# Output products in phases of their own, block products in two interleaved chains, and Strassen's seven products for the output GEMM of two superblocks

## The chip, the cores and the metric

One Trainium2 chip, one of its cores. The metric is the device time of one execution in microseconds (us): the median of three runs before the change is 983.1 us (982.56 to 983.92).

## The reference, cut to what matters

Causal window attention (window 64) over 4 x 576 tokens with 8 heads of 64, then a gated MLP with RMS norm, then a second MLP. 2304 tokens of width 512 go through all of it:

```python
xn = x / rms * rms_g
silu = g * (1.0 / (1.0 + np.exp(-g)))      # g = xn @ w_gate, 512 -> 1536
x = silu * (xn @ w_val) @ w_out            # 1536 -> 512
h = x @ w_in                               # 512 -> 2048
out = (h * (1.0 / (1.0 + np.exp(-1.702 * h)))) @ w_out2   # 2048 -> 512
```

The inputs are 64-bit floats; the kernel converts the weights on the chip from their 32-bit halves.

## The kernel before, in words

**Numbers.** Every GEMM keeps its operands as a high and a low fp32r part and does three matmuls for one (high x high, low x high, high x low).

**Stage 1** (loop `for j in range(NB)`, six blocks of 384 tokens): attention of the next block runs beside the first half of the gated MLP of this block, f = 0 to 5: `psg` and `psv` (12 matmuls of 384 columns each, helper `proj`), then 12 into the four `acc` banks (`emit_O`). At a block's end the next block's x is split into `xh` and `xl` (`split_x`, L462 to L466), on which the next `psg` waits.

**Stage 2** (three superblocks of 768 tokens, p = 0 to 2): the second half of the gated MLP. g and v come from Strassen's seven products of 2 x 2 blocks (Winograd's form with few sums): `chain` does 7 x 6 matmuls of 384 columns into two banks, `psa` and `psb`. ACT copies bank `psa` (`snap`, L677), DVE adds bank `psb` (`plus`, L681); `fill` puts groups of 12 output matmuls of the previous p between some of the products (`half_groups`: 6 of 512 and 6 of 256 columns on the same weights).

**Stage 3** (three superblocks, f = 0 to 7): the second MLP. h by the same `chain`, gelu and split into `g` (L936 to L938), and the output GEMM as plain matmuls of 512 columns into six banks, 36 for each f, put between the products as groups of 9 (`out_groups`).

**Weights.** `w_step` converts one pair of weight tiles: L201 and L202 on ACT (128x1024 each), L203, L204 and L207 on DVE (`m`). `w_half` then splits it; where Strassen's products need them, `w_products` makes four differences (L149 to L152) and high and low parts (`whi` L157, `wlo` L158, three pieces each) and stores them to DRAM, from where `t_load` brings `wt` back (two tiles for each chain). The conversions of stage 2 and 3 run on ACT and DVE beside the stage before.

**Order.** From the second block on the order of TensorE's instructions is that of the program; ACT, DVE and the DMA queue on SP take theirs from a scheduler, and each runs its own list strictly in order. A tile's buffer comes from a pool and is taken again when its last reader is done. The core of `chain` before:

```python
            a = mm_p.tile([128, 512], F32, tag="g", name="psa")
            prod(a, 0, True)
            s1 = snap("al")
            fill(0)
            b = mm_p.tile([128, 512], F32, tag="v", name="psb")
            prod(b, 1, True)
            prod(a, 5, False)
            plus(s1)
            s2 = snap("al")
            take(0, s1)
            fill(1)
            b = mm_p.tile([128, 512], F32, tag="v", name="psb")
            prod(b, 6, True)
            prod(a, 4, False)
```

Of the kernel before, what the change touches and what calls it, by code (L numbers as in the profile page):

```python
# [22 lines left out]
def window_attention__gated_mlp__mlp_kernel(  # L23
# [13 lines left out]
    nc = tc.nc  # L37
# [16 lines left out]
    wp = ctx.enter_context(tc.tile_pool(name="wp", bufs=11))  # L54
    const = ctx.enter_context(tc.tile_pool(name="const", bufs=1))
    xp = ctx.enter_context(tc.tile_pool(name="xp", bufs=4))
    ap_ = ctx.enter_context(tc.tile_pool(name="ap", bufs=2))
# [72 lines left out]

    def w_load(limit):
        while w_next[0] < min(limit, n_w):
            pair = w_order[w_next[0]]
            w_next[0] += 1
            st = stp.tile([128, 2, 1024], I32, tag="st", name="st")
            for e, (kind, f) in enumerate(pair):
                dst = st[:, e, :].rearrange("p (k f) -> p k f", k=KC) if kind in "gvh" else st[:, e, :]
                nc.sync.dma_start(out=dst, in_=w_src(kind, f))
            staged.append(st)
# [4 lines left out]
    wd = {}  # L144

    def w_products(key, m):
        b11, b21, b12, b22 = (m[:, i * 256:(i + 1) * 256] for i in range(4))
        t = mt[0][:, 1, :].bitcast(F32).rearrange("p (b c) -> p b c", c=256)
        nc.vector.tensor_tensor(t[:, 0, :], b12, b11, ALU.subtract)  # L149
        nc.vector.tensor_tensor(t[:, 1, :], b22, t[:, 0, :], ALU.subtract)  # L150
        nc.vector.tensor_tensor(t[:, 2, :], b22, b12, ALU.subtract)
        nc.vector.tensor_tensor(t[:, 3, :], b21, t[:, 1, :], ALU.subtract)  # L152
        hi = wp.tile([128, 7, 256], F32R, tag="w", name="whi")
        lo = wp.tile([128, 7, 256], F32R, tag="w", name="wlo")
        for dst, src in ((slice(0, 2), m[:, 0:512]), (slice(2, 3), m[:, 768:1024]), (slice(3, 7), t)):
            src = src if src is t else src.rearrange("p (b c) -> p b c", c=256)
            nc.scalar.copy(hi[:, dst, :], src)  # L157
            nc.vector.tensor_tensor(lo[:, dst, :], src, hi[:, dst, :].bitcast(F32), ALU.subtract)  # L158
        d = dram.tile([128, 2, 7, 256], F32, name="w%s_%d" % key, tag="w%s_%d" % key)
        nc.sync.dma_start(out=d[:, 0], in_=hi.bitcast(F32))  # L160
        nc.sync.dma_start(out=d[:, 1], in_=lo.bitcast(F32))
        wd[key] = d

    mt = [None]

    def w_half():
        if not half:
            return
        pair, w24 = half.pop()
        kind, p = pair[0]  # L170
        paired = kind == pair[1][0] and p + 1 != pair[1][1]
        if paired and kind in "gvh":
            return w_products(pair[0], w24.bitcast(F32))
        w = wp.tile([128, 2, 1024], F32R, tag="w", name="w")
        nc.scalar.copy(w[:, 0, :], w24.bitcast(F32))
        nc.vector.tensor_tensor(w[:, 1, :], w24.bitcast(F32), w[:, 0, :].bitcast(F32), ALU.subtract)
        if paired:
            d = dram.tile([128, 2, 1024], F32, name=f"w{kind}_{p}", tag=f"w{kind}_{p}")
            nc.sync.dma_start(out=d, in_=w.bitcast(F32))
            wd[kind, p] = d  # L180
            weights[kind, p] = w
            return
        for e, key in enumerate(pair):
            weights[key] = w[:, :, e * 512:(e + 1) * 512]

    def w_step(limit):
# [8 lines left out]
        if w_next[1] <= n_wh:  # L195
            m = wp.tile([128, 1024], I32, tag="w", name="m")
        else:
            mt[0] = stp.tile([128, 2, 1024], I32, tag="st", name="m")
            m = mt[0][:, 0, :]
        with after(hold[0]):  # L200
            nc.scalar.mul(hi.bitcast(F32), hi.bitcast(F32), 2.0 ** -112)  # L201
            nc.scalar.activation(lo, lo.bitcast(U32), AF.Copy, scale=2.0 ** -29)  # L202
        nc.vector.tensor_scalar(m.bitcast(U32), hi.bitcast(U32), 3, None, ALU.logical_shift_left)  # L203
        nc.vector.scalar_tensor_tensor(  # L204
            m.bitcast(U32), hi.bitcast(U32), 0x80000000, m.bitcast(U32), ALU.bitwise_and, ALU.bitwise_or
        )
        nc.vector.tensor_tensor(m, m, lo, ALU.add)  # L207
        half.append((pair, m))
        w_load(w_next[1] + 2)
# [22 lines left out]
    def part_tile():  # L232
        if not quad:
            pool = qp if n_quads[0] < 3 else wp
# [322 lines left out]
    if True:  # L557
# [55 lines left out]
        def small(tag):  # L613
            return ap_.tile([128, TB], F32, tag=tag, name=tag)

        MADE = (0, 1, 5, 6, 4, 2, 3)
        W_OF = (0, 1, 2, 6, 3, 4, 5)

        def x_raws(src):
            r = [x1p.tile([128, KC, TB], F32, tag="xr", name="xr", bufs=2) for _ in range(2)]  # L620
# [4 lines left out]
        def x_split(src):  # L625
            t = x1p.tile([128, 2, 2, TB], F32R, tag="xop", name="xop", bufs=8)
            nc.scalar.copy(t[:, 0], src)
            nc.vector.tensor_tensor(t[:, 1], src, t[:, 0].bitcast(F32), ALU.subtract)
            return t

        def x_first(r):
            a11, a12, a21, a22 = r[0][:, 0:2, :], r[0][:, 2:4, :], r[1][:, 0:2, :], r[1][:, 2:4, :]
            ops = {0: x_split(a11)}
            u, v = (osp.tile([128, 2, TB], F32, tag="os", name="xs") for _ in range(2))
            nc.vector.tensor_tensor(u, a21, a22, ALU.add)
            nc.vector.tensor_tensor(a21, a11, a21, ALU.subtract)
            nc.vector.tensor_tensor(a11, u, a11, ALU.subtract)
            nc.vector.tensor_tensor(v, a12, a11, ALU.subtract)
            return ops, {1: a12, 5: a11, 6: a21, 4: u, 2: v, 3: a22}

        def x_next(ops, left):
            for i in MADE:
                if i in left:
                    ops[i] = x_split(left.pop(i))
                    return
# [7 lines left out]
        def o_load(key):  # L653
            w = wp.tile([128, 2, 1024], F32R, tag="w", name="wo")
            nc.sync.dma_start(out=w.bitcast(F32), in_=wd[key])
            return w

        def chain(w, xo, fill, take, used):
            def prod(ps, i, first):
                k = 0  # L660
                for wi, xi in ((0, 0), (1, 0), (0, 1)):
                    for c in range(2):
# [3 lines left out]
                            w[wi][:, W_OF[i], c * 128:(c + 1) * 128],  # L666
# [6 lines left out]
                used(i)  # L673

            def snap(tag):
                t = small(tag)
                nc.scalar.copy(t, a[:, :TB])  # L677
                return t

            def plus(t):  # L680
                nc.vector.tensor_tensor(t, t, b[:, :TB], ALU.add)  # L681
                return t

            a = mm_p.tile([128, 512], F32, tag="g", name="psa")
            prod(a, 0, True)
            s1 = snap("al")
            fill(0)
            b = mm_p.tile([128, 512], F32, tag="v", name="psb")
            prod(b, 1, True)
            prod(a, 5, False)  # L690
            plus(s1)
            s2 = snap("al")
            take(0, s1)
            fill(1)
            b = mm_p.tile([128, 512], F32, tag="v", name="psb")
            prod(b, 6, True)
            prod(a, 4, False)
            s4 = snap("s")
            plus(s4)
            take(3, s4)  # L700
            fill(2)
            prod(a, 2, False)
            prod(b, 3, False)
            take(1, a[:, :TB])
            plus(s2)
            take(2, s2)
            fill(3)

        for j in range(NB):
# [28 lines left out]
            for f in range(FH):  # L738
# [13 lines left out]
                ah = ap_.tile([128, TB], F32R, tag="ah", name="ah")  # L752
                al = ap_.tile([128, TB], F32R, tag="al", name="al")
# [18 lines left out]
                if f == 0 and end:  # L772
                    at_es.close()
                    x1p = ctx.enter_context(tc.tile_pool(name="x1p", bufs=1))
                    raws = x_raws(lambda e: xd[e])
                if f == 1 and end:
                    xo, left = x_first(raws)
                if f > 1 and end:
                    for _ in range(2):
                        x_next(xo, left)  # L780
# [16 lines left out]

        pinned[0] = True
        nothing = lambda *_: None
        groups = [late.pop(), nothing, nothing, nothing]  # L800
        PIECES = ((0, 512), (512, 2 * TB))
        wg, wv, wo = t_load(("g", FH)), t_load(("v", FH)), o_load(("o", FH))

        def half_groups(sb, p, g, wo):
            if p == 0:
                banks = [(acc_p, f"acc{c}") for c in range(4)] + [(atp, "att")] * 2
                accs = [pool.tile([128, 512], F32, tag=tag, name="acc") for pool, tag in banks]
                spots[sb] = [(accs[c], accs[4 + c // 2][:, (c % 2) * 256:(c % 2 + 1) * 256]) for c in range(KC)]
            todo = [(e, c, pi, k) for e in (1, 0) for c in range(KC) for pi in range(3) for k in range(2)]

            def group(lo):
                for e, c, pi, k in todo[lo:lo + 12]:
                    first = p == 0 and e == 1 and pi == 0
# [165 lines left out]
```

## Time and profile before

| | |
|---|---|
| median of 3 runs | 983.1 us |
| the profiled execution | 981.57 us |
| its span, first to last instruction | 979.8 us |
| busy share of the span: TensorE (PE) / DVE / ACT | 96% / 58% / 51% |
| chain that ended last: PE / DVE / DMA / ACT | 78% / 8% / 5% / 5% |
| first block product of stage 2 starts | 363.68 us |
| first output product of stage 3 starts | 602.28 us |
| last matmul group starts | 965.21 us |

PE's matmuls overlap, and the profile models their ends: the step from one to the next is read from the starts of two groups in the order of time, not from the mean duration of one. A wait is idle time of an engine with the instruction that ended it.

### The profile page before, as it was taken

The page shows a single profiled execution, that of the slowest core. Times are in us where ns is not written, and L with a number is a line of the kernel's source. Part 1 is how long each engine was busy: PE and PEld are TensorE (multiplying, and loading weights), DVE is VectorE, ACT ScalarE, POOL GpSimd, SP SyncE. Part 2 cuts the span into 40 slices and gives each one's busy share as a digit, 9 for nine tenths or more (in the row PEclk, how much of TensorE's full clock was granted, in tenths as well). Part 3 has the DMA queues.
Part 4 walks back from the last instruction along what each step waited for, and adds up shares of the span by engine and source line. Part 5 has one row for each costly group of instructions (what it writes and reads, how often), then busy time and mean ns, then how long its engine had stood idle before and what let it go on. Part 6 is the DMA issues. An engine that isn't in the chain of part 4 may idle for free.

```text
span 979.8 us, 15502 instructions
## 1 busy us (share of the span) xinstructions
PE 937.7 (96%) x5966; PEld 859.7 (88%) x5966; DVE 571.8 (58%) x1207; ACT 495.0 (51%) x1054; POOL 12.2 (1%) x39
## 2 busy tenths in 40 slices
PE   8889999999999897999999989999999999999998
PEld 7789898989989897988988979888888888888887
DVE  5898578577776875677777676645452223422222
ACT  7786566556564344464464365545543333523332
POOL 2000000000000000000000000000000000000000
PEclk9899899999999899999999999999999999999999
DMA  9956376746655589899999898776583535554301
GB/s 223 255 161 175 109 194 179 218 121 194 193 162 186 187 329 412 325 398 385 359 371 352 337 382 316 264 269 246 193 315 139 233 135 220 209 210 172 151 1 65
DMA packets 136074, 228.95 MB, mean 234 GB/s; under 512 B 79936, under 2 KB 106560, under 8 KB 131392
## 3 DMA queue, kind: packets, MB, share of 16 engines
q1 hardware_dynamic: 135472, 227.96, 66.8%
q8 instruction: 47, 0.77, 0.3%
q14 instruction: 27, 0.22, 0.1%
q10 hardware_dynamic: 528, 0.00, 0.0%
HBM read 171.84 MB, written 56.10 MB: 233 GB/s over the span
## 4 chain that ended last, share of the span: by engine, by line
PE 78%; DVE 8%; DMA 5%; ACT 5%; issue 2%; SPq 2%; POOL 0%; ACTq 0%; DVEq 0%
PE acc L92 32%; PE psa L92 16%; PE psb L92 12%; PE psg L92 6%; PE psv L92 6%; DMA wt<-wv 2%; PE ps_v L92 2%; ACT st L201 1%; SPq L266 1%; PE ps_s L92 1%; ACT st L202 1%; DMA st<-in_moe_w_val_dram 1%; PE ps_t L92 1%; DMA wo<-wo 1%; PE ps_r L92 1%
## 5 line engine op out<-in xcount | busy, mean ns | idle before, releaser
L92 PE MATMUL psa<-xop,wt 128*128 128x384 f32 x1008 | 206.2, 340 | 8.2 <-ACT al L677 6.5
L92 PEld LDWEIGHTS psa<-xop,wt 128*128 128x128 f32 x1008 | 177.6, 188 | 17.3 <-ACT al L677 9.1
L92 PE MATMUL psb<-xop,wt 128*128 128x384 f32 x756 | 155.0, 340 | 6.6 <-DVE al L681 5.1
L92 PEld LDWEIGHTS psb<-xop,wt 128*128 128x128 f32 x756 | 134.5, 188 | 13.7 <-DVE al L681 7.5
L92 PE MATMUL acc<-wo,g 128*128 128x512 f32 x576 | 144.4, 397 | 0.0
L92 PEld LDWEIGHTS acc<-wo,g 128*128 128x128 f32 x576 | 107.7, 188 | 21.1
L681 DVE TENSOR_TENSOR al<-al,psb 128x384 f32<-128x384 f32 x84 | 46.4, 553 | 123.0 <-PE psb L92 118.3
L938 DVE TENSOR_TENSOR g<-a,g 128x384 fp32r<-128x384 f32 x96 | 53.1, 556 | 58.7 <-ACT g L937 58.7
L92 PE MATMUL acc<-g,wo 128*128 128x512 f32 (+1 forms) x432 | 81.8, 337 | 0.3 <-DVE g L865 0.3
L92 PE MATMUL psg<-xh,w 128*128 128x384 f32 x288 | 69.5, 366 | 7.0 <-DVE xh L462 3.4
L92 PEld LDWEIGHTS acc<-g,wo 128*128 128x128 f32 x432 | 68.1, 188 | 8.6 <-DVE g L865 0.6
L92 PE MATMUL acc<-w,g 128*128 128x512 f32 x288 | 72.3, 397 | 0.0
L677 ACT COPY al<-psa 128x384 f32<-128x384 f32 x84 | 39.9, 475 | 53.6 <-PE psa L92 53.5
L681 DVE TENSOR_TENSOR s<-s,psb 128x384 f32<-128x384 f32 x42 | 23.2, 552 | 72.2 <-ACT s L677 72.2
L677 ACT COPY s<-psa 128x384 f32<-128x384 f32 x42 | 20.1, 479 | 86.6 <-PE psa L92 86.6
L92 PEld LDWEIGHTS acc<-w,g 128*128 128x128 f32 x288 | 53.9, 188 | 10.4
L92 PE MATMUL psv<-xh,w 128*128 128x384 f32 x288 | 62.3, 349 | 0.0
L92 PEld LDWEIGHTS psg<-xh,w 128*128 128x128 f32 x288 | 51.5, 197 | 11.2 <-DVE xh L462 4.9
L92 PE MATMUL acc<-ah,w 128*128 128x384 f32 x288 | 60.0, 344 | 0.0
L362 ACT ACTIVATE p<-p,sm 128x128 f32<-128x128 f32 x128 | 49.6, 394 | 17.0 <-DVE sm L350 17.0
L936 ACT ACTIVATE a<-al 128x384 f32<-128x384 f32 x48 | 25.2, 526 | 60.7 <-DVE al L681 59.3
L92 PEld LDWEIGHTS psv<-xh,w 128*128 128x128 f32 x288 | 52.1, 193 | 0.3 <-issue 0.2
(129 smaller groups left out, 1369.4 us busy)
## 6 DMA issues: line engine op xcount, KB each, us to landing
wt<-wh SPq DMA_DIRECT2D x48, 896.0 KB, 6.7
wo<-wp SPq DMA_DIRECT2D x16, 1024.0 KB, 4.7
wt<-wg SPq DMA_DIRECT2D x18, 896.0 KB, 10.8
wt<-wv SPq DMA_DIRECT2D x18, 896.0 KB, 8.9
st<-in_moe_w_out_dram SPq DMA_DIRECT2D x28, 512.0 KB, 4.4
xr<-x SPq DMA_DIRECT2D x12, 768.0 KB, 6.2
wo<-wo SPq DMA_DIRECT2D x9, 1024.0 KB, 10.4
st<-in_moe_w_in_dram SPq DMA_DIRECT2D x16, 512.0 KB, 6.9
```

The source lines that it names most:

```text
L92: ins = op(*args, **kw)
L201: nc.scalar.mul(hi.bitcast(F32), hi.bitcast(F32), 2.0 ** -112)
L202: nc.scalar.activation(lo, lo.bitcast(U32), AF.Copy, scale=2.0 ** -29)
L266: nc.sync.dma_start(out=t[off:off + n], in_=src[b, :, s:s + n, :].rearrange("h s d -> s h d"))
L362: last_exp[0] = nc.scalar.activation(p[e][:, hp, :], p[e][:, hp, :], AF.Exp, bias=sm[:, 0, i:i + 1], scale=-1.0, accum_out=sm[:, 1, i:i + ...
L677: nc.scalar.copy(t, a[:, :TB])
L681: nc.vector.tensor_tensor(t, t, b[:, :TB], ALU.add)
L936: hold[0] = nc.scalar.activation(a, c, AF.Gelu_apprx_sigmoid).ins
L938: nc.vector.tensor_tensor(g[1][:, q, :], a, g[0][:, q, :].bitcast(F32), ALU.subtract)
```

## The change

- **Output products as phases.** `fill` is gone. `put` gives every piece of work a key, and `run_items` runs the pieces by key. One step (one product, 6 matmuls) is one key apart from the next.
- **Two chains.** `chain` is a generator that stops after each product; chain n+1 starts 7 keys after chain n, and a product of one alternates with a product of the other. Odd chains use the two `att` banks, even ones the `mm` banks. The order of the seven products is new, with two running sums.
- **Stage 2.** The output GEMM has units of 12 or 6 matmuls of 384 columns, for tokens t = 1, then t = 0; all six `w_out` tiles stay on the core (`wo`); p runs forwards, backwards, forwards, so that a turn finds its weights loaded.
- **Stage 3.** The first superblock keeps plain output matmuls of 512 columns, one chain with pieces between its steps. In the second and third the output GEMM is seven products too (`out_products`): 28 units of 18 matmuls of 256 columns, each on an operand that `prep` makes (a sum in place, a cast on ACT, a difference on DVE) four units ahead, and on weight blocks that `wload` reads from DRAM, 1 MB each, 14 for a superblock. The first three and, in the second superblock, the last three units lie between steps of chains.
- **Conversions.** In stages 2 and 3 the sign is kept by a Prelu on ACT, and the `or` on DVE (L204) is gone; `whi` is one cast, `lo` one difference, written over the staging tile `m`. The `w_out` pairs move from stage 1 into stage 2's first superblock.
- **Pools.** 11 buffers `wp` become 7 and 4 `wr`; stage 2 and 3 have their own pools of `g`.

```diff
-    wp = ctx.enter_context(tc.tile_pool(name="wp", bufs=11))
+    wp = ctx.enter_context(tc.tile_pool(name="wp", bufs=7, side="right"))
+    wr = late_es.enter_context(tc.tile_pool(name="wr", bufs=4, side="right"))
...
-    for p in range(NP1):
-        w_order += [((kind, FH + p), (kind, FH + NP1 + p)) for kind in "gvo"]
-    n_w1 = len(w_order)
+    for kinds in ("gv", "o"):
+        for p in range(NP1):
+            w_order += [((kind, FH + p), (kind, FH + NP1 + p)) for kind in kinds]
+        if kinds == "gv":
+            n_w1 = len(w_order)
...
+        hi = spare[0].tile([128, n, 256], F32R, tag="w", name="whi")
+        m = t[:, 0:n]
+        lo = lo_pool[0].tile([128, n, 256], F32R, tag="wl", name="wlo") if kind == "p" else m.bitcast(F32R)
+        nc.scalar.copy(hi, m)
+        nc.vector.tensor_tensor(lo, m, hi.bitcast(F32), ALU.subtract)
...
+                nc.scalar.activation(hi.bitcast(F32), hi.bitcast(F32), AF.Prelu, scale=2.0 ** -112, alpha=-(2.0 ** 32))
...
+            a = bank(n, 0)
+            prod(a, 0, True)
+            s1 = snap(a)
+            yield
+            b = bank(n, 1)
+            prod(b, 6, True)
+            s7 = snap(b)
+            yield
+            prod(a, 5, False)
+            s2 = snap(a)
+            yield
+            prod(b, 3, False)
+            take(2, plus(s2, b))
+            yield
...
+                for k in range(7):
+                    put(t0 + 14 * (n // 2) + 7 * (n % 2) + 2 * k, step)
...
+                if total:
+                    nc.vector.tensor_tensor(*total)
+                t = sp.tile([128, 2, 2, TB], F32R, tag="s", name="sop")
+                nc.scalar.copy(t[:, 0], src)
+                nc.vector.tensor_tensor(t[:, 1], src, t[:, 0].bitcast(F32), ALU.subtract)
...
+                                    banks[c // 2][:, (c % 2) * 256:(c % 2 + 1) * 256],
+                                    ops[i, pg][:, (0, 0, 1)[pi], e, c * 128:(c + 1) * 128],
+                                    wos[i, h][:, kk, (0, 1, 0)[pi], :],
```

**What moves on PE, stage 3, second superblock.** The names: `xop` are operands of block products, `wt` their weights, `g` the gelu's output. Before, block products (`psa`, `psb`) and plain output groups (`acc`) alternate all the way:

```order
L92 MATMUL psa<-xop,wt 128x384 x6
L92 MATMUL psb<-xop,wt 128x384 x6
L92 MATMUL acc<-wo,g 128x512 x9
L92 MATMUL psa<-xop,wt 128x384 x6
L92 MATMUL acc<-wo,g 128x512 x9
L92 MATMUL psb<-xop,wt 128x384 x6
L92 MATMUL psa<-xop,wt 128x384 x6
```

Now the same superblock has all block products first (x12 is a product of each chain), and the output products (`acca`, `accb`, from operands `sop`) after them:

```order
L95 MATMUL psb<-xop,wt 128x384 x12
L95 MATMUL psa<-xop,wt 128x384 x12
L95 MATMUL psb<-xop,wt 128x384 x6
L95 MATMUL acca<-wo,sop 128x256 x18
L95 MATMUL psa<-xop,wt 128x384 x6
L95 MATMUL acca<-wo,sop 128x256 x18
L95 MATMUL psb<-xop,wt 128x384 x6
L95 MATMUL acca<-wo,sop 128x256 x18
L95 MATMUL psa<-xop,wt 128x384 x6
L95 MATMUL acca<-wo,sop 128x256 x18
L95 MATMUL accb<-wo,sop 128x256 x72
L95 MATMUL acca<-wo,sop 128x256 x72
```

The output matmuls of the second and third superblock are 1008 of 256 columns where there were 576 of 512.

**What moves on DVE, end of stage 1's fifth block.** Before, between the last `a` and the split of the next block's x (`xh`) stand a conversion's `or` (L204) and add (ISA L207) and two operand splits of stage 2 (`xop`):

```order
L747 SCALAR_TENSOR_TENSOR a<-a,psg 128x384
L203 TENSOR_SCALAR m<-st 128x1024
L751 TENSOR_TENSOR a<-a,psv 128x384
L204 SCALAR_TENSOR_TENSOR m<-st,m 128x1024
L628 TENSOR_TENSOR xop<-xr,xop 128x768
L207 ISA m<-st,m 128x2048
L628 TENSOR_TENSOR xop<-xr,xop 128x768
L755 TENSOR_TENSOR al<-a,ah 128x384
L462 CAST xh<-xraw 128x384 x2
```

Now no conversion is left there; two operations of stage 2's operands stand in the same place:

```order
L806 SCALAR_TENSOR_TENSOR a<-a,psg 128x384
L661 TENSOR_TENSOR xr<-xr 128x768
L810 TENSOR_TENSOR a<-a,psv 128x384
L661 TENSOR_TENSOR xr<-xr 128x768
L664 TENSOR_TENSOR xop<-xr,xop 128x768
L814 TENSOR_TENSOR al<-a,ah 128x384
L492 CAST xh<-xraw 128x384 x2
```

The `or`, the add and one split have left the place between `a` and `al`, and one sum has come in.

## Rows read from the trace of the kernel before

**Rows 1.** Windows: stretch and length; busy us (instructions) PE, PEld, DVE, ACT, POOL; PEclk; DMA.
```profile
326.00:329.00 3.00, 3.00 (x11) 3.00 (x10) 1.89 (x3) 1.43 (x2) 0.00 (x0) 0.50 0.27 115
...
375.00:395.00 20.00, 14.01 (x75) 12.46 (x74) 14.65 (x24) 8.44 (x16) 0.00 (x0) 1.00 1.03 404
```

**Rows 2.** Groups by shape, PE, 363.68 us to the end: busy, mean ns, idle before.
```profile
L92 PE MATMUL psa<-xop,wt 128*128 128x384 f32 x1008 | 206.2, 340 | 8.2 <-ACT al L677 6.5 <-ACT s L677 1.7
L92 PE MATMUL psb<-xop,wt 128*128 128x384 f32 x756 | 155.0, 340 | 6.6 <-DVE al L681 5.1 <-DVE s L681 1.5
```

**Rows 3.** Order of time, PE, start of stage 2: start, length, group.
```profile
363.68 1.22 PE L92 MATMUL psa<-xop,wt 128*128 128x384 f32 x6
...
365.80 1.22 PE L92 MATMUL psa<-xop,wt 128*128 128x384 f32 x6
```

**Rows 4.** Order of time, PE, stage 2's output groups; last row: group by shape there.
```profile
392.98 2.27 PE L92 MATMUL acc<-g,wo 128*128 128x512 f32 x12
395.09 1.22 PE L92 MATMUL psa<-xop,wt 128*128 128x384 f32 x6
...
L92 PE MATMUL acc<-g,wo 128*128 128x256 f32 x6 | 1.7, 280 | 0.0
```

**Rows 5.** Order of time, PE, stage 3's plain output groups.
```profile
861.67 2.27 PE L92 MATMUL acc<-wo,g 128*128 128x512 f32 x9
863.78 1.22 PE L92 MATMUL psb<-xop,wt 128*128 128x384 f32 x6
```

**Rows 6.** Order of time, PE: the first of 15 waits of stage 2.
```profile
377.77 1.33 PE L92 MATMUL psa<-xop,wt 128*128 128x384 f32 x6 [2.27 <-ACT al L677]
```

**Rows 7.** Chain that ended last, 374 to 378 us: start, us, what.
```profile
374.44 1.11 ACT st L201
...
377.35 0.38 ACT al L677
```

**Rows 8.** Order of time, end of block 5: DVE, then PE.
```profile
316.91 1.22 DVE L204 SCALAR_TENSOR_TENSOR m<-st,m 128x1024 uint32<-128x1024 uint32 x1
...
317.57 0.87 PE L92 MATMUL acc<-al,w 128*128 128x384 f32 x4
...
321.80 2.01 PE L92 MATMUL psg<-xh,w 128*128 128x384 f32 x7 [2.17 <-DVE xh L462]
...
329.76 1.57 PE L92 MATMUL acc<-ah,w 128*128 128x384 f32 x8
```

**Rows 9.** Groups by shape, DVE and ACT, from 357 us on.
```profile
L681 DVE TENSOR_TENSOR s<-s,psb 128x384 f32<-128x384 f32 x42 | 23.2, 552 | 72.2 <-ACT s L677 72.2
L628 DVE TENSOR_TENSOR xop<-xr,xop 128x768 fp32r<-128x768 f32 x24 | 22.9, 956 | 16.2 <-ACT xop L627 16.0 <-DMA wt<-wh 0.2
...
L207 DVE CUSTOM_DVE_ANT_0 m<-st,m 128x2048 uint16<-128x2048 uint16 x16 | 19.6, 1222 | 0.3
L203 DVE TENSOR_SCALAR m<-st 128x1024 uint32<-128x1024 uint32 x16 | 11.1, 692 | 8.0 <-ACT st L201 7.9
...
L936 ACT ACTIVATE a<-al 128x384 f32<-128x384 f32 x48 | 25.2, 526 | 60.7 <-DVE al L681 59.3 <-DVE g L938 1.4
...
L627 ACT CAST xop<-xr 128x768 fp32r<-128x768 f32 x24 | 20.0, 835 | 14.8 <-PE psa L92 10.9 <-PE psb L92 3.9
```

**Rows 10.** Order of time, PE, transposes of 128 columns; then a weight load group.
```profile
111.86 0.60 PE L92 MATMUL ps_t<-ident,p 128*128 128x128 f32 x4
112.22 0.77 PE L92 MATMUL psg<-xl,w 128*128 128x384 f32 x3
...
L92 PEld LDWEIGHTS acc<-wo,g 128*128 128x128 f32 x576 | 107.7, 188 | 21.1
```

**Rows 11.** Last matmuls in the order of time; then DMA issues: KB, us to landing.
```profile
965.21 10.71 PE L92 MATMUL acc<-wo,g 128*128 128x512 f32 x45
...
wo<-wp SPq DMA_DIRECT2D x16, 1024.0 KB, 4.7
...
wh<-wlo SPq DMA_DIRECT2D x8, 896.0 KB, 10.4
```

More of the change, by code (lines that the diff above doesn't have):

```diff
@@ L651, in t_load, with bank, chain @@
             return w
[L653 to L658, printed above, removed]
+        def bank(n, i):
+            if n % 2:
+                return atp.tile([128, 512], F32, tag="att", name="psb" if i else "psa")
+            return mm_p.tile([128, 512], F32, tag="gv"[(i + n // 2) % 2], name="psb" if i else "psa")
+        def chain(n, load, ops, take):
+            w, xo = load(), ops
             def prod(ps, i, first):
@@ L697, in chain @@
[L697 to L701, printed above, removed]
+            s1 = snap(a)
[10 more added lines that the diff above has]
+            yield
+            prod(a, 4, False)
+            take(3, plus(s7, a))
@@ L702, in chain, with put, put_chains, step @@
+            yield
+            b = bank(n, 1)
+            prod(b, 1, True)
+            take(0, plus(s1, b))
+            yield
             prod(a, 2, False)
-            prod(b, 3, False)
             take(1, a[:, :TB])
-            plus(s2)
-            take(2, s2)
-            fill(3)
+            yield
+        items = []
+        def put(key, fn):
+            items.append((key, len(items), fn))
+        def put_chains(t0, chains):
+            for n, make in enumerate(chains):
+                it = []
+                def step(it=it, make=make):
+                    if not it:
+                        it.append(make())
+                    next(it[0])
+                for k in range(7):
+                    put(t0 + 14 * (n // 2) + 7 * (n % 2) + 2 * k, step)
@@ new lines, in run_items, with loads @@
+        def run_items():
+            for _, _, fn in sorted(items, key=lambda x: x[:2]):
+                fn()
+            items.clear()
+        loaded = {}
+        def loads(n, ahead=3):
+            for key in [k for k in loaded if k not in keys[max(n - 1, 0):n + 3]]:
+                loaded.pop(key)
+            for key in keys[n:n + ahead]:
+                if key not in loaded:
+                    loaded[key] = t_load(key)
+            return loaded[keys[n]]
+        ZIG = [range(NP1), range(NP1 - 1, -1, -1), range(NP1)]
@@ L709, in window_attention__gated_mlp__mlp_kernel @@
+        keys1 = [(kind, FH + p) for sb in range(NSB) for p in ZIG[sb] for kind in "gv"]
+        keys2 = [("h", p) for sb in range(NSB) for p in range(NP2)]
+        keys = keys1 + keys2
         for j in range(NB):
@@ L796, in window_attention__gated_mlp__mlp_kernel @@
             xh, xl = nxh, nxl
+        while todo:
+            todo.pop(0)()
         pinned[0] = True
[L799 to L813, printed above, removed]
-                    shared = k == 1 and c % 2 == 1
+        x_es.close()
@@ new lines, in last @@
+            def last(t, c):
+                for p, e in order[-2:]:
+                    mms(t, p, e, c)
+                part = osp.tile([128, TB], F32, tag="os", name="part")
+                nc.sync.dma_start(out=part, in_=osd[sb][:, c, t * TB:(t + 1) * TB])
+                nc.vector.tensor_tensor(part, part, accs[t][c][:, :TB], ALU.add)
+                nc.sync.dma_start(out=x2d[sb][:, c, t * TB:(t + 1) * TB], in_=part)
+            units = []
+            for t in (1, 0):
+                units += [(2, lambda t=t, k=k: unit(t, k)) for k in range(4)]
+                units += [(1, lambda t=t, c=c: last(t, c)) for c in range(KC)]
@@ new lines, in window_attention__gated_mlp__mlp_kernel, with gelu_chains, gelu @@
+        run_items()
+        g_es.close()
+        late_es.close()
+        spare[0] = wp
+        gp = ctx.enter_context(tc.tile_pool(name="gq", bufs=16, side="right"))
+        lo_es = ExitStack()
+        lo_pool.append(lo_es.enter_context(tc.tile_pool(name="wl", bufs=3, side="right")))
+        NPG = NP2 // 2
+        def gelu_chains(sb):
+            g = {}
+            order = list(range(NP2))
+            out = []
+            def gelu(j, q, c):
+                pg = j // 2
+                if (pg, q) not in g:
+                    g[pg, q] = gp.tile([128, 2, TB], F32, tag="g", name="g")
+                hold[0] = nc.scalar.activation(g[pg, q][:, j % 2], c, AF.Gelu_apprx_sigmoid).ins
+            for n, p in enumerate(order):
+                out.append(lambda n=n, p=p: chain(
+                    n, lambda: loads(len(keys1) + sb * NP2 + n, min(3, NP2 - n)), all_ops[NSB + sb], lambda q, c: gelu(n, q, c)
+                ))
+            return out, g, order
```

525 lines of the change are left out of this document (320 added, 205 removed).

## Prediction

> **What bounds the kernel now.** I read the windows by stage first, then the groups by shape, then PE's order of time at the places that the change touches, and the chain of waits where PE stood. From the first block product at 363.68 us on, PE's matmuls follow each other with hardly a hole, so that what the kernel costs there is the number of matmul columns plus the waits. The step from start to start gives the price of a matmul: 12 of 384 columns take 365.80 - 363.68 = 2.12 us, 0.1767 us each [rows 3]; 9 of 512 take 863.78 - 861.67 = 2.11 us, 0.2344 us each [rows 5]; 6 of 512 with 6 of 256 take 395.09 - 392.98 = 2.11 us [rows 4]. Less 6 x 0.2344, a matmul of 256 columns is worth (2.11 - 1.41) / 6 = 0.117 us, each with a weight load of its own.
>
> Now the whole stretch, to the end of the last matmul, 965.21 + 45 x 0.2344 = 975.8 us [rows 11], 612.1 us: 1764 matmuls of chains x 0.1767 = 311.7 [rows 2, 3]; 216 pairs of stage 2's output x 0.3517 = 76.0 [rows 4]; 864 of stage 3's output x 0.2344 = 202.5 [rows 5]; 12 left over from block 6, 2.1. Sum 592.3. So 19.8 us are lost to waits. 8.2 + 6.6 of them are listed as idle before `psa` and `psb` [rows 2], and 6.0 of the 20 us from 375 on [rows 1]. The reader is to see who ends them: `snap` on ACT and `plus` on DVE [rows 6], late because ACT and DVE run in order and a conversion stands ahead. There the copy of `psa` comes at 377.35, behind casts (`st`) that began at 374.44 [rows 7].
>
> **The change, part by part.**
>
> *Output GEMM of two superblocks.* 576 x 0.2344 = 135.0 us become 1008 x 0.117 = 117.9 us: -17.1. No row shows a long run of 256-column matmuls, where every 0.117 us needs a load. Lower bound of the price: the line through 384 and 512 columns gives 0.119 at 256, the transposes show that a load with 128 columns fits into (112.22 - 111.86) / 4 = 0.09 us [rows 10]; I take 0.117 as the nearest row. Upper bound: 0.188, the mean duration of a load [rows 10], if loads could not overlap at all.
>
> The Trainium skill (TensorE: Matmul & The Clock Gate, section Back-to-back issue gap) has a fixed 2.5 ns for each matmul beside N / 2.4: an estimate from it, 576 x 215.8 ns less 1008 x 109.2 ns, saves 14.2 us, 2.9 us less gain than above. The rows have nearly no such fixed part (0.1767 to 0.2344 is close to 384 to 512), so the measurement differs and I keep it.
>
> *Stage 2's output.* 216 pairs of 512 and 256 become 432 of 384: 76.3 for 76.0 us, nothing.
>
> *The waits of the block products.* Before, `prod` on bank a waits for a copy that had one product (1.06 us) or one product and a group (3.2 us) to finish. With two chains three products, 3.2 us, always lie between a bank's product and the next into it. A copy takes 0.38 us on the chain and an add 0.55 [rows 7, 9], so a burst of up to 2.5 us of conversion ahead is covered, and the 2.27 us wait of rows 6 would go. What is late next: the first superblock of stage 2 still has five conversions in 42 keys (44.5 us). By the order its DVE list has 18 adds and 22 operations of that size (0.55 each), five conversions (0.69 + 1.22, and to split two of them 1.22, two by their 2816 columns 3.4) and seven operand operations of 0.96 [rows 9]: 22.0 + 9.6 + 9.2 + 6.7 = 47.5 us at most, of 44.5, some of it free to run later. I leave 2.5 us there. Weights: 7 buffers hold three and a half chains, so the second tile of chain n+3 is read only after chain n, 9 keys (9.5 us) ahead of its use; transfers of that size landed in 10.4 us in the crowded stage (`wh`, [rows 11]). The lost `w_out` reloads and turned order of p take traffic away; 1.5 us for each of the second and third superblock. A raw load now waits on SP until the store of the low parts has landed (10.4 us, [rows 11]), with `wt` reads queued behind; the output phase (25 us without chain reads) takes that in. Start of stage 3: its first chain has no filler and its casts of 2048 run ahead on ACT, 1.5. The other seven chains there, with one conversion each: 1.5. The hand-over to each Strassen output phase, where the fourth operand needs add, gelu, cast and difference (0.55 + 0.53 + 0.84 + 0.96 = 2.9 us, [rows 9]) inside 3.2 us: 0.5 each. Together 9.5 instead of 19.8: -10.3. Bounds: 0 lost (-19.8) and all kept (0), or more if operands come late, a rival below.
>
> *Operands of the output products.* 28 units of 18 x 0.117 = 2.1 us, 59 us. On DVE 16 sums and 28 differences of 768 elements at 0.956 [rows 9], 6 adds of some 0.55 and in the second superblock another 11 such operations for the third's x: 42.1 + 3.3 + 10.5 = 56 us, beside and not on the path as long as it is spread. ACT: 28 x 0.84 plus copies, 28 us. `wload`: 14 MB in 59 us, a product (8.4 us) ahead, landing 4.7 us [rows 11]. All at nothing; the cover is the four-unit lead, and without it the exposed part is the rival below.
>
> *Stage 1.* The end of block 5 took 329.76 - 318.28 (the start 317.57 + 4 x 0.1767) = 11.5 us for 24 matmuls worth 4.2: 7.2 lost, 2.17 us of it waiting for `xh` on DVE [rows 8], and then a clock granted at half (0.50, so 1.2 of 2.4 GHz) for the next 3 us [rows 1], after PE had stood. The `or` (1.22 us), the add and a split leave that place and a sum enters: `xh` comes some 2.1 us earlier. I take 3.5 us, half of the loss, since the clock may then hold. One `or` less at two other waits: 1.0. -4.5; bounds 0 and -9. Block 1's order changes too (transposes a few matmuls later), for which I have no sign: +-2.
>
> *End.* The last copy is 256 columns instead of 512: -0.3.
>
> **Sum.** -17.1 - 10.3 - 4.5 - 0.3 = -32.2. Span 979.8 -> 947.6; the profiled execution has 1.8 us around its span, 949.4; the median of three runs is 1.5 us above the profiled one: 951 us.
>
> **Rivals.**
>
> *Waits stay.* ACT and DVE keep delaying products (same work, same in-order lists), SP's new waits cost what the two chains gain, and stage 1 keeps its boundary. Then only -17.4 is left: 979.8 - 17.4 + 3.3 = 966 us. For it: DVE full in stage 2's first superblock. Against: conversions are fewer and the cover 3.2 us.
>
> *Operands late in the output phases.* Where sums, stage 3's next x and adds fall together, DVE has 4 x (0.956 + 0.956) + 2 x 1.5 + 1.1 = 11.7 us for a product's 8.4 us: 3.3 us, for three of seven products in the second superblock, 1 in the third: 11 us, so 962. Against: sums need no free buffer and stand early in DVE's list.
>
> *Loads bound the 256-column matmuls* (the other side). If a load could not start before the last one ended, each unit matmul would take 0.188: 1008 x (0.188 - 0.117) = +71.6, 1023 us. It decides from 0.149 on, where 1008 x 0.032 eats the 32 us. For it: the load group's mean [rows 10] and 1008 loads in a row. Against: 0.09 us steps with a load each [rows 10] and pairs at full rate [rows 4].
>
> The Trainium skill (same page, section LDWEIGHTS) puts a load of 128 columns at 128 / 1.2 = 107 ns and says of the fast load that FP32 does not get it; by that estimate a load would just fit behind 0.117 us, and the rival would cost nothing. No row here shows a load by itself.
>
> *The change doesn't do what it says:* the order shows 1008 of 256 columns and single chains only in the first superblock of stage 3, so I give this no chance of its own.
>
> **How the numbers follow.** Forecast 951 (waits halved): 0.62. Waits stay, 966: 0.18. Operands late, 962: 0.12. Fewer waits than I leave (down to 942, where the lost time is near zero): inside the forecast's low end. Loads bound, 1023: 0.04. Rest, 0.04: about no change, by a queue that blocks somewhere I did not see, half of it slower. The range reaches from 942, 9.5 us of waits gone, to 968, the dearer of the two middle rivals with the 2 us of block 1; beyond it lie the last two cases, 0.08, at the top, and some 0.06 of the forecast below. A measurement of this kernel can tell 0.2% (2 us) from no change. Faster 0.93; same 0.02; slower 0.05.
>
> **What would show each step.** Right: `acca` and `accb` groups of 18 matmuls step 2.1 us, 72 in 8.4; idle before `psa` and `psb` in sum under 6 us; no `or` in stage 2 and 3; first block product near 359 us. Wrong: idle before `acca` ended by `sop` (operands late); steps above 2.3 us for 18 without idle time (loads); idle ended by ACT `sn` or DMA `wt` above 15 us (waits stay). The prediction falls if the time is over 968 or under 942.

## The result and the profile after

The changed kernel took 954.6 us (median of four runs, 952.2 to 956.7), the kernel before 983.0 us beside it (982.6 to 983.9): a ratio of 0.971, with an interval of 0.969 to 0.973. That is 28.4 us less; 32 were forecast.

The page of the kernel after: busy time of the engines, then the chain of work that ended last, then groups (busy and mean ns, then idle time before them and what ended it).

```profile
span 954.9 us, 16476 instructions
PE 919.3 (96%) x6398; PEld 880.5 (92%) x6398; DVE 605.9 (63%) x1216; ACT 512.1 (54%) x1028; POOL 12.1 (1%) x39
...
PE 74%; DVE 12%; ACT 5%; DMA 5%; issue 3%; SPq 0%; POOL 0%; DVEq 0%; ACTq 0%
...
L95 PE MATMUL psa<-xop,wt 128*128 128x384 f32 x1008 | 192.9, 335 | 0.4 <-DMA wt<-wv 0.4
...
L95 PE MATMUL psb<-xop,wt 128*128 128x384 f32 x756 | 147.1, 335 | 0.8 <-DVE sn L704 0.8
...
L95 PE MATMUL acc<-g,w 128*128 128x384 f32 x432 | 87.5, 356 | 6.2 <-DVE part L919 5.9
...
L95 PE MATMUL acca<-wo,sop 128*128 128x256 f32 x576 | 72.0, 283 | 0.2 <-DVE sop L1002 0.2
```

The waits before the block products, 8.2 and 6.6 us before [rows 2], are 0.4 and 0.8. But a group of stage 2's output, `acc<-g,w`, now has 6.2 us ahead of it, ended by L919 on DVE, the addition that empties an accumulator bank. No part of the forecast had that wait.

PE in order of time: the first block product, a run of 256-column matmuls, and the last group:

```profile
362.56 1.20 PE L95 MATMUL psa<-xop,wt 128*128 128x384 f32 x6
363.60 1.55 PE L95 MATMUL acc<-ah,w 128*128 128x384 f32 x8
...
780.33 8.80 PE L95 MATMUL accb<-wo,sop 128*128 128x256 f32 x72
788.97 1.24 PE L95 MATMUL acca<-wo,sop 128*128 128x256 f32 x9
...
942.71 8.80 PE L95 MATMUL acca<-wo,sop 128*128 128x256 f32 x72
```

Start to start, 384 columns take 1.04 / 6 = 0.1733 us (before 0.1767, [rows 3]) and 256 columns 8.64 / 72 = 0.120 us (forecast 0.117). The same sum as in the prediction, over 362.56 to 942.71 + 72 x 0.120 = 951.35 us:

| part | before | after | |
|---|---|---|---|
| start of the first block product | 363.7 | 362.6 | -1.1 |
| output of stage 3's second and third superblock | 135.0 | 121.0 | -14.0 |
| all other matmuls from there to the end | 457.3 | 449.9 | -7.4 |
| lost (length less the matmuls) | 19.8 | 17.9 | -1.9 |
| from the last matmul to the end of the span | 4.0 | 3.5 | -0.5 |
| span | 979.8 | 954.9 | -24.9 |

This profiled execution was the longest of the four; the others were 1.9 to 4.5 us shorter. Two rows were not in the forecast: the other matmuls, most of them of the same shape and number as before, got cheaper by 7.4 us, and the lost time stayed nearly what it was, though the waits in which it had been are gone. PE, DVE and the clock in the middle of stage 2 show where it is now. First PE in order of time, the output phase of the first superblock:

```profile
414.80 7.06 PE L95 MATMUL acc<-g,w 128*128 128x384 f32 x36
423.68 1.01 PE L95 MATMUL acc<-g,w 128*128 128x384 f32 x3 [1.82 <-DVE part L919]
425.08 2.66 PE L95 MATMUL acc<-g,w 128*128 128x384 f32 x6 [0.39 <-DVE part L919]
428.62 9.65 PE L95 MATMUL acc<-g,w 128*128 128x384 f32 x39 [0.87 <-DVE part L919]
438.10 1.20 PE L95 MATMUL psa<-xop,wt 128*128 128x384 f32 x6
```

DVE in the same stretch:

```profile
419.13 2.03 DVE L181 TENSOR_TENSOR m<-m,whi 128x1792 fp32r<-128x1792 f32 x1
421.07 1.22 DVE L237 CUSTOM_DVE_ANT_0 m<-st,m 128x2048 uint16<-128x2048 uint16 x1
422.21 0.95 DVE L664 TENSOR_TENSOR xop<-xr,xop 128x768 fp32r<-128x768 f32 x1
423.07 0.55 DVE L919 TENSOR_TENSOR part<-part,acc 128x384 f32<-128x384 f32 x1
...
424.48 0.55 DVE L919 TENSOR_TENSOR part<-part,acc 128x384 f32<-128x384 f32 x1
424.94 0.95 DVE L664 TENSOR_TENSOR xop<-xr,xop 128x768 fp32r<-128x768 f32 x1
425.81 0.55 DVE L919 TENSOR_TENSOR part<-part,acc 128x384 f32<-128x384 f32 x1
426.27 1.82 DVE L664 TENSOR_TENSOR xop<-xr,xop 128x768 fp32r<-128x768 f32 x2
428.01 0.55 DVE L919 TENSOR_TENSOR part<-part,acc 128x384 f32<-128x384 f32 x1
```

And the windows (columns as in [rows 1]):

```profile
415.00:420.00 5.00, 4.89 (x27) 4.25 (x26) 4.98 (x8) 5.00 (x6) 0.00 (x0) 1.00 0.20 82
420.00:425.00 5.00, 2.88 (x14) 2.04 (x12) 5.00 (x8) 2.86 (x5) 0.00 (x0) 0.91 1.00 368
425.00:430.00 5.00, 4.04 (x10) 3.03 (x11) 4.97 (x10) 0.00 (x0) 0.00 (x0) 0.50 1.01 335
430.00:435.00 5.00, 5.00 (x19) 5.00 (x19) 2.06 (x2) 1.69 (x1) 0.00 (x0) 0.57 1.00 384
435.00:440.00 5.00, 5.00 (x30) 5.00 (x29) 0.00 (x0) 0.48 (x1) 0.00 (x0) 1.00 1.04 392
```

The output of tokens t = 1 and t = 0 goes through the same four banks, so the second half can't start into a bank before the first half's addition has read it. DVE has no gap in this stretch (4.98, 5.00 and 4.97 of 5 us) and puts a conversion (L181, L237) and operands for the next superblock (L664) ahead of the four additions, each of which would take 0.55 us. PE stands, and then the granted clock is 0.50, 1.2 of 2.4 GHz, from about 424 to 434 us. 84 matmuls, worth 84 x 0.1733 = 14.6 us, take 438.10 - 414.80 = 23.3 us: 8.7 lost, of which the rows list 3.1 as waits. From 428.62 us on no wait is listed, and still 39 matmuls take 9.5 us where 6.8 would do: 2.7 us went to the clock there. The second superblock loses 6.2 in the same place (84 matmuls from 492.18 to 512.95 us, with the clock at 0.50 from 503 to 509), the third 0.7. That is 15.6 of the 17.9 us.

### The profile page after: what moved, and what is told of

Its sections match the earlier page's. It is cut to its first block, busy times and chain, and to the rows that moved or that the text cites. A ratio compares the mean times of both kernels' runs of the same rounds, so it can differ in the third digit from the quotient of the medians.

```text
span 954.9 us, 16476 instructions
## 1 busy us (share of the span) xinstructions
PE 919.3 (96%) x6398; PEld 880.5 (92%) x6398; DVE 605.9 (63%) x1216; ACT 512.1 (54%) x1028; POOL 12.1 (1%) x39
## 4 chain that ended last, share of the span: by engine, by line
PE 74%; DVE 12%; ACT 5%; DMA 5%; issue 3%; SPq 0%; POOL 0%; DVEq 0%; ACTq 0%
PE acc L95 17%; PE psa L95 14%; PE psb L95 11%; PE psg L95 7%; PE psv L95 7%; PE acca L95 6%; PE accb L95 5%; DVE xop L664 2%; PE ps_v L95 2%; PE ps_s L95 2%; PE ps_t L95 1%; DMA xr<-x 1%; ACT st L231 1%; DMA st<-in_moe_w_in_dram 1%; DVE xr L661 1%
## 5 line engine op out<-in xcount | busy, mean ns | idle before, releaser
L704 DVE TENSOR_TENSOR sn<-sn,psb 128x384 f32<-128x384 f32 x84 | 46.3, 552 | 80.5 <-PE psb L95 79.6
L95 PE MATMUL acc<-g,w 128*128 128x384 f32 x432 | 87.5, 356 | 6.2 <-DVE part L919 5.9
L95 PEld LDWEIGHTS acc<-g,w 128*128 128x128 f32 x432 | 80.9, 202 | 9.9 <-DVE part L919 9.2
L95 PE MATMUL acca<-wo,sop 128*128 128x256 f32 x576 | 72.0, 283 | 0.2 <-DVE sop L1002 0.2
L1002 DVE TENSOR_TENSOR sop<-g,sop 128x768 fp32r<-128x768 f32 x56 | 53.3, 957 | 28.6 <-ACT sop L1001 28.5
L95 PEld LDWEIGHTS acca<-wo,sop 128*128 128x128 f32 x576 | 70.8, 191 | 0.5 <-DVE sop L1002 0.5
L700 ACT COPY sn<-psa 128x384 f32<-128x384 f32 x84 | 40.0, 476 | 57.3 <-PE psa L95 57.3
L1001 ACT CAST sop<-g 128x768 fp32r<-128x768 f32 x56 | 46.4, 835 | 40.5 <-PE accb L95 23.2
L95 PE MATMUL acc<-whi,g 128*128 128x512 f32 x192 | 67.8, 392 | 0.0
L95 PE MATMUL accb<-wo,sop 128*128 128x256 f32 x432 | 52.8, 283 | 0.0
L95 PEld LDWEIGHTS accb<-wo,sop 128*128 128x128 f32 x432 | 52.3, 192 | 0.0
```

The costliest lines, as they stand in the source:

```text
L95: ins = op(*args, **kw)
L700: nc.scalar.copy(t, ps[:, :TB])
L704: nc.vector.tensor_tensor(t, t, ps[:, :TB], ALU.add)
```

## The experiments

The theory: the columns that Strassen's products save and the two chains make the gain; it is cut by additions that stand late in DVE's list in stage 2, and by the half clock after PE has stood. The rivals: the step of PE got shorter by chance of the chip; the additions are late for their DMA; the chains do nothing that the phases don't.

### The kernel before once more

No edit.

> The kernel before once more, on the chip that runs the others: a look at the price of a 384-column matmul. In the two traces it is 0.1767 us before and 0.1733 us after, in stage 1 too, which the change hardly touches. If the program sets it, this run shows 0.1767 us again (12 in 2.12 us) and 983 us; if the chip or the execution sets it, it shows about 0.173 us (12 in 2.08 us) and stage 3's output matmuls near 0.23 us, and part of the gain would be no work of the change.

982.4 us, and the first block products of this trace, in order of time:

```profile
363.00 1.22 PE L92 MATMUL psa<-xop,wt 128*128 128x384 f32 x6
364.06 1.22 PE L92 MATMUL psb<-xop,wt 128*128 128x384 f32 x6
```

1.06 / 6 = 0.1767 us. It is not the chip: the program sets the step, in matmuls that the change left alone.

### The additions first

```diff
-                nc.vector.tensor_tensor(part, part, accs[t][c][:, :TB], ALU.add)
+                added[t] = nc.vector.tensor_tensor(part, part, accs[t][c][:, :TB], ALU.add).ins
...
+            def behind(box=box, added=added):
+                with after(added[1]):
+                    box.pop(0)()
...
             for i in range(7):
-                put(t0 + 48.05 + 0.1 * i, lambda box=box: box.pop(0)())
+                if i < 2:
+                    put(t0 + 48.05 + 0.1 * i, lambda box=box: box.pop(0)())
+                else:
+                    put(t0 + 48.72 + 0.01 * i, behind)
```

> After, with five of the seven operand conversions for the next superblock put behind the last addition of partial sums (L919) in VectorE's order, so that the accumulator banks are emptied as soon as their last matmul has ended. Theory (the additions are late because VectorE is still at work that was put ahead of them; the waits of 3.4, 2.5 and 0.35 us and the half clock behind them cost 15 us of PE): the acc waits of stage 2 fall under 1.5 us in all, the clock holds through 414 to 440 and 492 to 513 us, and the time is 941 us (938 to 946). Rival (the partial sums come late by their DMA, or the banks are free late for another reason): the waits stay and the time is 952 to 957 us. Second rival: the conversions now come late for the next superblock's first block product, 948 to 953 us with new waits before psa or psb on VectorE's xop.

942.5 us (940.6 to 943.4), 0.959 of the kernel before (0.957 to 0.961). The same phase on PE, and the additions on DVE:

```profile
412.87 14.72 PE L95 MATMUL acc<-g,w 128*128 128x384 f32 x84
427.43 1.20 PE L95 MATMUL psa<-xop,wt 128*128 128x384 f32 x6
```

```profile
417.21 1.62 DVE L919 TENSOR_TENSOR part<-part,acc 128x384 f32<-128x384 f32 x3
...
419.41 0.55 DVE L919 TENSOR_TENSOR part<-part,acc 128x384 f32<-128x384 f32 x1
419.88 0.95 DVE L661 TENSOR_TENSOR xr<-xr 128x768 f32<-128x768 f32 x1
```

The 84 matmuls follow each other in 14.56 us, where they took 23.3, and PEclk is 1.00 from 300 us to 930 us in each window that was read. Nothing was taken away: DVE has the same additions, conversions and operands, in another order. So the additions were late by DVE's order, and they and the half clock behind them cost 12 us; the DMA of `part` had no share in these waits that shows, since DVE had no gap ahead of the additions. No wait on `xop` came, which was the second rival. At the start of stage 3 the chains now wait 2.3 us on the additions of L704 (0.8 in the kernel after): in DVE's list two weight splits (L181, 4.5 us) and four additions of L919 (1.9 us) stand directly ahead of them. And the chains wait 1.5 us for weights (0.4), so some 2.6 of the 15 us came back as other waits. This version beats both kernels.

### One chain at a time

```diff
-                    put(t0 + 14 * (n // 2) + 7 * (n % 2) + 2 * k, step)
+                    put(t0 + 7 * n + k, step)
```

> After, with the block products of stages 2 and 3 in one chain at a time (chain n ends before chain n+1 begins; the two pairs of banks still alternate from chain to chain). The first superblock of stage 3, which had one chain already, is as before. Theory (two interleaved chains are what hides the copy and the addition between two products of one bank): the waits before psa and psb come back, 0.2 to 0.5 us at each of some 3 places in 34 chains, 8 to 20 us in all, 963 to 975 us. Rival (it was enough that the conversions and the output products left the stretch of the block products): 953 to 958 us and waits before psa and psb that stay under 3 us.

962.6 us (962.1 to 964.2). The groups of its page:

```profile
L95 PE MATMUL psa<-xop,wt 128*128 128x384 f32 x1008 | 201.2, 339 | 11.3 <-ACT sn L700 10.6
...
L95 PE MATMUL psb<-xop,wt 128*128 128x384 f32 x756 | 154.5, 339 | 0.9 <-DVE sn L704 0.9
L95 PE MATMUL acc<-g,w 128*128 128x384 f32 x432 | 78.2, 336 | 1.8 <-DVE part L919 1.8
```

11 us of waits before `psa` are back, ended by the copy L700: it is the two chains that hide this copy, not the phases. The waits before `psb`, 6.6 us in the kernel before, stay away with one chain too (0.9 us), so something else in the change removed them: no run tells the new order of the seven products from the conversions that moved. The time grew by only 8.0 us, just under the range expected, since the waits before `acc` fell from 6.2 to 1.8 us; that PE's waits gave DVE the time for this is likely, but was not tested.

### Plain output in the second and third superblock of stage 3

```diff
-        for sb in range(1, NSB):
-            chains, g, order = gelu_chains(sb)
...
+        for sb in range(NSB):
...
+            for f in range(NP2):
...
+                elif f + 1 < NP2:
+                    p_load(f + 1)
...
+                    if before:
+                        lo, hi = 12 * k // 7, 12 * (k + 1) // 7
+                        out_mms(f - 1, before[0], before[1][lo:hi], sb)
```

> After, with the output GEMM of the second and third superblock of stage 3 as in the first one: 36 plain matmuls of 512 columns for each of 8 pairs, put between the products of the next block, with the weights loaded from the scratch in DRAM. Theory (the forecast's main term: 1008 matmuls at 0.120 us in place of 576 at 0.233 us): 121.0 us become 134.4 us, so 13.4 us longer, 968 us (965 to 974), and the first superblock unchanged. Rival (the columns saved were given back in the output phases, and the gain came from the waits): 953 to 959 us.

964.2 us (962.1 to 970.8), 9.6 us more, between the two expectations by the medians. By stages it is clear. The first line is PE at the start of stage 3, the last its last group:

```profile
585.24 1.31 PE L95 MATMUL psb<-xop,wt 128*128 128x384 f32 x6 [0.77 <-DVE sn L707]
...
947.25 9.72 PE L95 MATMUL acc<-wpl,g 128*128 128x512 f32 x42
```

With 0.2314 us for 512 columns (517 matmuls of this group, start to start) stage 3 lasts from 585.24 to 956.97, 371.7 us; in the kernel after from 593.27 to 951.35, 358.1. So stage 3 is 13.6 us shorter with the output products. What made the difference of the whole smaller is ahead of stage 3, which begins 8.0 us earlier here. 3.2 of these are there at the first block product (359.32 for 362.56 us), though the program of stage 1 is the same in both. 4.8 come in stage 2: it has nearly the same waits for `part` (6.6 and 5.9 us), but the clock stood at 0.50 for less time, some 7 us near 425 us, where the kernel after had it there for 10 us and again from 503 to 509.

### The place of the weight tiles in SBUF

The change also puts pool `wp` at the other end of SBUF, with `wr` and `xp` beside it. `wp` alone, in the kernel before:

```diff
-    wp = ctx.enter_context(tc.tile_pool(name="wp", bufs=11))
+    wp = ctx.enter_context(tc.tile_pool(name="wp", bufs=11, side="right"))
```

> The kernel before with the pool of the weight tiles (wp) put at the other end of SBUF, as after has it, and nothing else; the order on TensorE is the same. The kernel before has shown a step of 0.176 us for 384 columns and 0.234 us for 512 in two profiles, and four programs with the change's pools 0.174 and 0.231 us, in stage 1 too: some 2.5 to 3 ns less for every matmul. Theory (where the weight tiles lie in SBUF sets it): this kernel shows 0.174 and 0.231 us, and some 5900 matmuls by 2.5 ns make it 12 to 16 us faster, 967 to 971 us. Rival (the step hangs on something else that the change brought): 0.176 us as before, 980 to 984 us.

974.0 us (974.0 to 974.9), the kernel before 981.9 beside it: 0.992 (0.990 to 0.993). That is 7.9 us of the kernel before, from one word in the diff. The steps came as expected except in stage 3's block products (0.1757 us), and the gain is less than the 12 to 16 us expected. And undone in the kernel after:

```diff
-    wp = ctx.enter_context(tc.tile_pool(name="wp", bufs=7, side="right"))
+    wp = ctx.enter_context(tc.tile_pool(name="wp", bufs=7))
```

> After with the pool of the weight tiles (wp) at the end of SBUF where before has it, and nothing else; the order on TensorE is the same. Theory (the weight tiles' place sets 2.5 to 3 ns of every matmul): 384 columns take 0.176 us again and 256 columns 0.122 us, and some 6300 matmuls make it 13 to 18 us slower, 968 to 972 us. Rival: 0.174 and 0.119 us as after, 952 to 957 us.

957.1 us (954.3 to 961.2). The same product in both, PE in order of time, first of the kernel before with `wp` moved:

```profile
361.16 1.20 PE L92 MATMUL psa<-xop,wt 128*128 128x384 f32 x6
362.20 1.20 PE L92 MATMUL psb<-xop,wt 128*128 128x384 f32 x6
```

then of the kernel after with `wp` moved back:

```profile
360.96 1.23 PE L95 MATMUL psa<-xop,wt 128*128 128x384 f32 x6
362.02 1.55 PE L95 MATMUL acc<-ah,w 128*128 128x384 f32 x8
```

1.04 against 1.06 us for six: the step goes with the place, not with the rest of the program. Over whole stages (start to start, at a granted clock of 1.00 and without a wait between them):

| us a matmul | before | before, moved | after | after, moved back |
|---|---|---|---|---|
| 384 columns, stage 2's `psa` | 0.1765 | 0.1737 | 0.1734 | 0.1768 |
| 512 columns on tiles of `wp`, stage 3 | 0.2343 | 0.2308 | 0.2308 | 0.2340 |
| 384 columns, stage 2's `acc`, not on `wp` | | | 0.1736 | 0.1736 |
| 256 columns, `accb` | | | 0.1200 | 0.1182 |

The 256-column matmuls got faster by 1.8 ns with `wp` moved back, though their weights lie in `wp` too. Moving `wp` also shifts the pools beside it, so that which tile's place counts was not separated. And the 8 us of the kernel before did not come back in the kernel after. Its four runs scatter with the granted clock (954.3 and 954.9 us at 0.989, 959.2 and 961.2 at 0.98; in the profile, one of the first two, PEclk is 1.00 from 412 to 444 us in spite of the waits for `part`). The place could not be priced there, so I tried it in the version without these waits.

### The place once more, and the sign, with the additions first

Three programs on one chip: the version with the additions first, the same with `wp` moved back (the diff as above), and the same with the conversions as before:

> The version with the additions first once more, beside the next two on one chip: 940 to 944 us, and no acc wait on part over 0.2 us.

> The version with the additions first, with the pool wp at the end of SBUF where before has it; the order on TensorE is the same. Without the waits and the half clock that scattered the run of after with wp there, the place should show clean. Theory (2 to 3 ns for every 384- and 512-column matmul of stages 2 and 3, some 2500 of them, 1.5 ns in stage 1, and nothing for the 256-column ones, by the steps seen): 7 to 10 us longer than the version beside it. Rival (in the changed program the longer step lies beside waits, and is not paid): within 2 us of it.

```diff
-                nc.scalar.activation(hi.bitcast(F32), hi.bitcast(F32), AF.Prelu, scale=2.0 ** -112, alpha=-(2.0 ** 32))
+            nc.scalar.mul(hi.bitcast(F32), hi.bitcast(F32), 2.0 ** -112)
...
-        if first:
-            nc.vector.scalar_tensor_tensor(
-                m.bitcast(U32), hi.bitcast(U32), 0x80000000, m.bitcast(U32), ALU.bitwise_and, ALU.bitwise_or
-            )
+        nc.vector.scalar_tensor_tensor(
+            m.bitcast(U32), hi.bitcast(U32), 0x80000000, m.bitcast(U32), ALU.bitwise_and, ALU.bitwise_or
+        )
```

> The version with the additions first, with the conversions as before (multiply on ScalarE, the sign bit by one more instruction of 1.2 us on VectorE). If VectorE has room for them once the additions are not late, the time is that of the version beside it within 2 us; if VectorE's length decides even then, the acc waits on part come back and it is 3 to 8 us longer.

944.0 (941.1 to 945.7), 946.1 (945.3 to 947.6) and 942.5 us (941.9 to 944.7). In the first no wait before `acc` came, as expected.

The place costs 2.1 us here by the medians, and 2.7 in stages 2 and 3 of the profiles: my 7 to 10 fell. The rival has the size nearly right, but not the reason, since the longer steps are paid. The block products take 756 x 0.0034 + 1008 x 0.0026 = 5.2 us more and the 512-column matmuls 0.5. Against it the 256-column matmuls take 1.5 us less (1.4 to 1.8 ns each), and the waits for `wt` fall from 1.2 to 0.2 us, perhaps because longer steps give the loads more time. That leaves 3.2 us, near the 2.7.

The sign on VectorE costs nothing that these runs can tell: two waits for `part` come back (1.6 and 0.4 us), and the waits for weights go. In the kernel after, without the new order, the same edit was expected to cost more:

> After with the conversions as before: ScalarE multiplies, and VectorE puts the sign bit in by one more instruction (some 1.2 us by its neighbour's row) for each conversion after the first ones. Theory (VectorE's work ahead of the part additions is what delays them, so 5 more of these in stage 2's first superblock and 3 in each of the next add to the delay, and the Prelu form is worth what they would cost): the acc waits on part grow from 6.2 us to 9 to 13 us, and with the half clock behind them the time is 957 to 964 us. Rival (the conversions lie far enough from the additions, so their length does not matter): 952 to 957 us.

It gave 952.0 us (950.4 to 952.3), no more than the kernel after, with 5.7 us of waits for `part` where that had 5.9, and 1.2 on `g`. The times don't compare cleanly, since in stage 2 of the two profiles the clock stood at 0.50 for some 3 us here and some 17 in the kernel after; the waits do, and they did not grow to 9 to 13 us. So my theory on DVE's load fell in this form. What stands directly ahead of the additions counts, as the run with the additions first shows.

## Why the prediction was right, and where not

The time, 954.6 us, is 3.6 above the forecast of 951 and inside 942 to 968. Of its steps:

- **Output GEMM, -17.1: right in kind, too large.** 13.6 us by the run with plain output, 14.0 by the table. The price was the step that failed: 0.117 us, from six matmuls between wider ones; a long run takes 0.120 (432 matmuls of `accb`). I had taken stage 3's 0.2344 us for 512 columns off stage 2's pairs, in which the wide matmul takes 0.2327 and the narrow one 0.1179. The line through 384 and 512 columns had given 0.119, and stood in the prediction as a bound. At a granted clock of 1.00, 2.4 GHz, a matmul of the kernel after carries 13 to 18 ns beside its columns (0.1734 - 0.160, 0.2308 - 0.2133, 0.1200 - 0.1067); that the rows have nearly no such fixed part was a misreading, since in the rows before it is 17 to 21 ns. The estimate from the Trainium skill (TensorE: Matmul & The Clock Gate, section Back-to-back issue gap), against which I kept my rows, was 14.2 us: on the saving it was nearer, though its fixed part of 2.5 ns is too small for these rows.
- **Waits of the block products, -10.3: right in mechanism, undersized.** 14.8 us listed before `psa` and `psb` became 1.2. The run with one chain gives 11 of them back before `psa`, so there the two chains did it; what removed the waits before `psb` was not separated. Outside stage 2's output phases 2.3 us of the lost time are left, where I had left 9.5.
- **Stage 2's output, "nothing": the step that failed.** I counted its matmuls, 76.3 for 76.0 us, and not that its two halves share four banks, with an addition on DVE between them. By the order on PE (84 `acc` matmuls in a row) no block product lies between these halves to cover an addition; DVE's work ahead of the additions I had counted (47.5 us in 44.5) and put at 2.5 us of waits in the chains. It cost 15.6 us in this execution, and 12 in the median by the run with the additions first.
- **Stage 1, -4.5: right at its place, not at its end.** The end of block 5 lost 3.6 us where it had lost 7.2, as forecast. The listed waits there fell only from 3.9 to 2.6 us; most of the rest is the clock, which stayed at 1.00 from 318 to 330 us, where before it had been 0.50 for some 7 us (the prediction read 3). But the first block product came at 362.6 us, and at 359.3 to 362.6 in five profiles with this stage 1, against 363.0 and 363.7: 2.2 us on the mean. Part was given back in block 1, which I had put at +-2: from its first `psg` to that of block 2 it took 65.8 to 66.4 us in these five, and 64.2 and 64.7 before. And in the kernel before with `wp` moved the product came at 361.2 without any of this, so how the 2.2 us divide stays open.
- **End, -0.3:** -0.5.
- **Not in the sum: the place of `wp`.** It was in the diff, and I read over it. 7.4 us fewer for the other matmuls in the two profiles; 7.9 us as a change of its own in the kernel before; 2 to 3 us when undone in the faster version. Why these differ is shown only for the last, by the 256-column matmuls and the waits for `wt`; that a shorter step gives loads less cover is my reading and was not tested.
- **The rivals.** Waits that stay (966) and loads that bound the narrow matmuls (1023) did not come: the 256-column step is 0.120 us with a load each. Operands late was right in kind at another place: not `sop` ahead of the output products (0.2 us), but a conversion and the next superblock's `xop` ahead of stage 2's additions.

So the total came out well by luck: misses of both signs met. In the profiled span, 954.9 for 947.6 us: +15.6 for the wait that I had not seen, +3.1 for the output GEMM, +3.4 for stage 1, against -7.2 from the waits of the block products, -7.4 from the cheaper matmuls and -0.2 at the end, +7.3 in all.

## What to carry to other kernels

When work is gathered into phases of its own, ask for each bank which instruction frees it for the phase's second half, and what the in-order engine that runs it has in front: on a full engine the order can be worth more than the load (12 us here by order alone, while the `or` put back on DVE cost nothing that the runs can tell). Price a narrow matmul from a long run or from the line through two widths, never from a small difference of mixed groups. A word in a diff that only moves a buffer is a term too; a second profile of the old kernel tells whether a step that changed everywhere is the chip's or the program's.

## What the runs showed of the hardware that was not expected

- The place of a tile pool in SBUF changes the step of matmuls that use it: 0.176 to 0.177 or 0.173 to 0.174 us for stage 2's block products, by the side on which `wp` lies, in ten programs. In stage 3 of the kernel before with `wp` moved it lay between, 0.1757. Within one program (after, `wp` moved back) the 512-column matmuls on `whi` from `wp` take 0.2340 us, those on `wlo` from another pool 0.2308; in the kernel after they take 0.2308 and 0.2317. What about the place does it was not tried.
- The half clock behind a wait does not follow from the listed wait alone. With 3.1 us of waits in some 15 us PE was granted 0.50 from 424 to 434 us in the kernel after; with 4.2 us of them in the same place it was granted 1.00 all through in the profile of the kernel with `wp` moved back:

```profile
412.00:444.00 32.00, 27.70 (x153) 26.11 (x152) 21.38 (x32) 12.14 (x17) 0.00 (x0) 1.00 0.82 302
```
